# A fused attention and expert kernel: half tiles for the experts' x, and another order around the first two experts

## The chip, the cores and the metric

The kernel runs on one core of one Trainium2 chip. The metric is the device time of one execution in microseconds (us). Five engines work side by side, each through its own queue in order: TensorE (PE, whose weight loads are listed as PEld), VectorE (DVE), ScalarE (ACT), GpSimd (POOL) and SyncE (SP, which only issues DMAs here). They wait for one another through semaphores.

## The reference

Three stages follow one another, and only the last one is touched by the change.

```python
# stage 1: a linear attention with a decaying state, 4 x 8 heads, 768 steps, head size 48
# stage 2, on 3072 tokens of width 384
x = ((x @ w1) * (x @ w2)) @ w3 @ w_out
# stage 3: 8 experts, the best two for each token
noisy = x @ w_gate + log1p(exp(x @ w_noise)) * noise
top2 = argpartition(-noisy, 2)[:, :2]
top2_w = softmax(noisy[top2])
for e in range(8):
    h = maximum(x[mask_e] @ moe2_w1[e], 0)
    out[mask_e] += top2_w * (h @ moe2_w2[e])
```

## The kernel before, in words

The 3072 tokens are 24 chunks of 128, worked on in 12 groups of two. Attention of later chunks is interleaved with the projection of earlier groups: `mo_ab` makes the product of the two projections in four pieces (fp = 0 to 3), `mo_x` multiplies a piece by the folded w3·w_out (with the gate's 16 columns appended) into two banks of the accumulator memory, one for each chunk, and `mo_out` empties the banks: a copy of the gate's logits into `LZ` by DVE, a copy of x into `xo` by ACT, and a DMA of `xo` to a table of rows in memory. `gate_top` and `gate_put` turn the logits of four chunks into places (`slots`) in the experts' lists and write them there from POOL.

Every product is made of three matmuls (`mm3`, lines 171 to 173): each f32 operand is a rounded high part (h, a cast by ACT) and a rest (l, a subtraction by DVE), and h·h, h·l and l·h are added up.

An expert has up to 800 tokens in two halves: half 0 is four tiles of 128, half 1 is two tiles of 128 and a last one of 32. `load_idx` reads an expert's list (`ti`), `gather` fetches its rows (`xg`), `turn` writes them to `expert_rows` and reads them back through a transposing DMA into the tile `XTx` (for expert 0's first half the tile `XTa`), and `tr` splits that into `XTh` (three casts by ACT, line 749) and `XTl` (three subtractions by DVE, line 750). `mm1(hf, ff)` makes column block ff of the hidden layer from them, with a Relu by ACT and a rest by DVE behind it, and `mm2(e, j)` the output of tile j, which ACT scales (`ye`, line 799) and POOL adds to the output by an indirect DMA. `split_e(e, m, i)` splits quarter i of an expert's first (m = 0, `WAh`, `WAl`) or second (m = 1, `WBh`, `WBl`) weight matrix. The accumulator banks are `pb_66` to `pb_73`.

In the kernel before, `XTh`, `XTl` and, from expert 1 on, `XTx` are one tile each of 800 columns, and a half is a slice of it. For expert 0's second half the rows come too late for the way through memory; `tr_pe` joins them on DVE (`join`) and transposes them with nine matmuls on PE, put in the middle of the last of half 0's four `mm2`.

What sets the order: DVE's instructions stay in the order in which the program names them (`manual_schedule`). On the other engines a scheduler may move an instruction ahead of others that wait longer; one in `keep_in_program_order` stays behind the one that the program names just ahead of it on its engine, though later ones may still overtake it. So are kept all DMAs of SP, the casts of `tr`, and the casts of `split_e` for experts from 1 on. An instruction waits for every earlier one of the program whose tiles it needs, as the scheduler sees the overlap of the slices.

Around the change the program reads: last group, in whose steps i = 7 and i = 11 stand `turn(0, 0)` and `tr(0, 0)`; the last `mo_x` and `mo_out`; eight `mm1` of expert 0's half 0 with the last four chunks' gate in between (lines 898 to 916); four `mm2` with `tr_pe`; eight `mm1` of half 1; `turn(1, 0)` and `turn(1, 1)`; `mm2` of tiles 4, 6 and 5 with expert 1's first weights split behind them, and `tr(1, 0)` after tile 5 (j == NT - 2); then the loop over experts 1 to 7. In expert 1's first half, `turn(2, 0)` stands at ff = 3 and `tr(1, 1)` right behind it.

Of the kernel before, what the change touches and what calls it, by code (L numbers as in the profile page):

```python
# [18 lines left out]
P = 128  # L19
# [52 lines left out]
def tile_kernel(ctx: ExitStack, tc: tile.TileContext, dt, nat, w3t, wout, w1, w2, e1, e2, cf, ci, out):  # L72
# [462 lines left out]
    def mo_out(g):  # L535
        for tt in range(2):
            t = 2 * g + tt
            dve.tensor_copy(out=LZ[:, t, :], in_=bX[tt][:, DM:XW])
            xo = work.tile([P, 2 * DM], U16, name="xo")
            act.copy(out=halves(xo), in_=bX[tt][:, :DM].bitcast(U16).rearrange("p (d t) -> p t d", t=2))  # L540
            act.dma_start(out=x2d[DUMP + t * P:DUMP + P + t * P], in_=xo)
# [133 lines left out]
    def open_a():  # L675
        EP["a"] = ctx.enter_context(tc.tile_pool(name="epa", bufs=1))
        XT["h"] = EP["a"].tile([P, 3, CAP], F32R, name="XTh")
        XT["l"] = EP["a"].tile([P, 3, CAP], F32R, name="XTl")
        XT["x"] = EP["a"].tile([P, 3, NAB[0]], F32, name="XTa")
        open_h(EP["a"], 0)  # L680
# [9 lines left out]
    def open_b():  # L690
        EP["b"] = ctx.enter_context(tc.tile_pool(name="epb", bufs=1, side="right"))
        open_h(EP["b"], 1)
        XT["x"] = EP["b"].tile([P, 3, CAP], F32, name="XTx")
# [9 lines left out]
    def split_e(e, m, i):  # L703
        s = slice(768 * i, 768 * i + 768)
        o = 768 * (i % 2)
        src = RW[e, m, i // 2][:, o:o + 768]
        h, l = (WAh, WBh)[m][:, s], (WAl, WBl)[m][:, s]
        cast = act.copy(out=h, in_=src)  # L708
        if e:
            tc.keep_in_program_order(cast)  # L710
        dve.tensor_tensor(out=l, in0=src, in1=f(h), op=OP.subtract)
# [23 lines left out]
    def turn(e, hf):  # L735

        for j in range(TA) if hf == 0 else range(TA, NT):
            tc.keep_in_program_order(sp.dma_start(
                out=rows[e % 2, 2 * TPT * j:2 * TPT * j + 2 * rows_of(j)].rearrange("(p t) d -> p (t d)", t=2),
                in_=XG[e, j][:rows_of(j)]))  # L740
        a = 2 * hf * NAB[0]
        s = slice(a, a + 2 * NAB[hf])
        tc.keep_in_program_order(sp.dma_start_transpose(out=XT["x"].bitcast(U16)[:, :, s], in_=rows[e % 2, s]))

    def tr(e, hf):
        s = slice(hf * NAB[0], hf * NAB[0] + NAB[hf])
        for db in range(3):
            x, h = XT["x"][:, db, s], XT["h"][:, db, s]
            tc.keep_in_program_order(act.copy(out=h, in_=x))  # L749
            dve.tensor_tensor(out=XT["l"][:, db, s], in0=x, in1=f(h), op=OP.subtract)  # L750
# [7 lines left out]
    def tr_pe():  # L758
        for j in range(TA, NT):
            join(j)  # L760
        s = slice(NAB[0], NAB[0] + NAB[1])
        for db in range(3):
# [4 lines left out]
            split(XT["h"][:, db, s], XT["l"][:, db, s], bank[:, :NAB[1]])  # L767
# [4 lines left out]
    def mm1(hf, ff, banks=None):  # L772
        n = NAB[hf]
        s0 = hf * NAB[0]
        banks = banks or MB[:2 + hf]
        bank = banks[ff % len(banks)][:, :n]
        for kb in range(3):
            w = slice(kb * FF + ff * P, kb * FF + ff * P + P)
            mm3(bank, WAh[:, w], WAl[:, w], XT["h"][:, kb, s0:s0 + n], XT["l"][:, kb, s0:s0 + n], kb == 0, kb == 2)
# [60 lines left out]
    def first_half(e, r):  # L840
# [5 lines left out]
        for ff in range(8):  # L846
            mm1(0, ff)
            if ff in (3, 6) and e + 1 < E:
                turn(e + 1, ff // 6)
            if e == 1 and ff == 3:  # L850
                tr(1, 1)
# [20 lines left out]
    for g in range(NGRP):  # L872
# [7 lines left out]
        for i in range(12):  # L880
            if g == NGRP - 1 and i == 7:
                turn(0, 0)
            if g == NGRP - 1 and i == 11:
                tr(0, 0)
# [3 lines left out]
            elif g:  # L888
                mo_x(g - 1, 3)
                mo_out(g - 1)  # L890
# [12 lines left out]
    low_p()  # L903
    mo_x(NGRP - 1, 3)
    mo_out(NGRP - 1)
# [3 lines left out]
    for ff in range(8):  # L909
        for _ in range((5, 1, 0, 2, 1)[ff] if ff < 5 else 1):  # L910
            next(gen, None)
        mm1(0, ff, (bA, bB, PB[4], PB[5]))
# [21 lines left out]
    for i, j in enumerate((TA, NT - 1, *range(TA + 1, NT - 1))):  # L934
        mm2(0, j)
        split_e(1, 0, i)
        if j == NT - 2:
# [130 lines left out]
```

## Time and profile before

| what | us |
|---|---|
| median of 3 runs (lowest, highest) | 940.91 (940.27, 942.82) |
| the profiled execution, time | 944.25 |
| its span, which the views count in | 942.5 |
| PE busy in it | 902.0 (96%) |
| DVE busy | 493.0 (52%) |
| ACT busy | 429.6 (46%) |
| POOL busy | 243.6 (26%) |

The mean granted clock of PE over the span is 0.98 of its full speed. Matmuls are pipelined: a row's duration runs from its start to its modelled end, and the next one starts before that, so the pace of PE is read from the distance of starts. A row's bracket says how long the engine sat idle before it and which instruction ended that.

### The profile page before, as it was taken

The page shows a single profiled execution, that of the slowest core. Times are in us where ns is not written, and L with a number is a line of the kernel's source. Part 1 is how long each engine was busy: PE and PEld are TensorE (multiplying, and loading weights), DVE is VectorE, ACT ScalarE, POOL GpSimd, SP SyncE. Part 2 cuts the span into 40 slices and gives each one's busy share as a digit, 9 for nine tenths or more (in the row PEclk, how much of TensorE's full clock was granted, in tenths as well). Part 3 has the DMA queues.
Part 4 walks back from the last instruction along what each step waited for, and adds up shares of the span by engine and source line. Part 5 has one row for each costly group of instructions (what it writes and reads, how often), then busy time and mean ns, then how long its engine had stood idle before and what let it go on. Part 6 is the DMA issues. An engine that isn't in the chain of part 4 may idle for free.

```text
span 942.5 us, 17579 instructions
## 1 busy us (share of the span) xinstructions
PE 902.0 (96%) x7076; PEld 834.2 (89%) x7076; DVE 493.0 (52%) x1177; ACT 429.6 (46%) x875; POOL 243.6 (26%) x218
## 2 busy tenths in 40 slices
PE   8998999999999999999989978999999999999994
PEld 6787799999999999999978857989898999989894
DVE  5887874756756666655344344353343434353430
ACT  6777556456456545644451333343334343343320
POOL 2100001041141231231405540704224160613112
PEclk9998999999999999999999898999999999999998
DMA  9946377254253442420332982846748283854212
GB/s 355 363 143 209 134 86 218 88 133 163 97 166 122 136 127 80 125 80 19 105 97 88 184 257 60 241 103 167 178 117 210 76 213 73 224 120 95 26 21 36
DMA packets 96827, 130.41 MB, mean 138 GB/s; under 512 B 56064, under 2 KB 76768, under 8 KB 96736
## 3 DMA queue, kind: packets, MB, share of 16 engines
q1 hardware_dynamic: 81120, 104.76, 37.5%
q0 software_dynamic: 12160, 19.72, 11.1%
q10 hardware_dynamic: 3456, 4.72, 1.4%
q8 instruction: 57, 0.93, 0.4%
q14 instruction: 34, 0.28, 0.1%
HBM read 88.12 MB, written 31.66 MB: 127 GB/s over the span
## 4 chain that ended last, share of the span: by engine, by line
PE 78%; DVE 6%; issue 6%; DMA 5%; ACT 2%; POOL 2%; POOLq 0%; SPq 0%; DVEq 0%; ACTq 0%
PE pb L171 23%; PE pb L172 23%; PE pb L173 23%; PE pb L309 3%; PE pb L249 2%; DMA ti<-slots 1%; PE pb L804 1%; PE pb L270 1%; POOL slots L646 1%; DVE cvz L155 1%; PE pb L259 1%; DMA xg<-x_rows,ti 1%; ACT top L146 1%; DMA raw<-w 1%; POOL xg L732 1%
## 5 line engine op out<-in xcount | busy, mean ns | idle before, releaser
L809 POOL DMA_INDIRECT out<-ye,ti x56 | 89.1, 1592 | 255.4 <-ACT ye L799 231.6
L171 PE MATMUL pb<-XTh,WAh 128*128 128x512 f32 (+1 forms) x384 | 134.6, 351 | 10.5 <-ACT XTh L749 9.9
L172 PE MATMUL pb<-XTl,WAh 128*128 128x512 f32 (+1 forms) x384 | 133.5, 348 | 0.6 <-DVE XTl L750 0.6
L173 PE MATMUL pb<-XTh,WAl 128*128 128x512 f32 (+1 forms) x384 | 132.0, 346 | 0.0
L171 PE MATMUL pb<-WBh,HH 128*128 128x384 f32 x384 | 131.3, 342 | 0.4 <-ACT WBh L708 0.4
L173 PE MATMUL pb<-WBh,HH 128*128 128x384 f32 x384 | 130.4, 340 | 0.0
L172 PE MATMUL pb<-WBl,HH 128*128 128x384 f32 x384 | 130.3, 339 | 0.0
L781 ACT ACTIVATE HH<-pb 128x512 fp32r<-128x512 f32 (+1 forms) x128 | 62.8, 492 | 120.4 <-PE pb L173 118.8
L782 DVE SCALAR_TENSOR_TENSOR HH<-pb,HH 128x256 fp32r<-128x256 f32 (+1 forms) x128 | 71.1, 557 | 88.7 <-ACT HH L781 88.7
L799 ACT ACTIVATE ye<-pb,ti 128x384 f32<-128x384 f32 x48 | 27.9, 582 | 151.8 <-PE pb L173 112.7
L646 POOL DMA_INDIRECT slots<-g_sc,g_si x48 | 51.5, 1074 | 167.3 <-DVE g_si L645 85.2
L171 PEld LDWEIGHTS pb<-XTh,WAh 128*128 128x128 f32 x384 | 73.2, 191 | 21.0 <-ACT XTh L749 10.8
L171 PE MATMUL pb<-xh,WAh 128*128 128x256 f32 x288 | 82.3, 286 | 3.4 <-DVE W1l L125 3.1
L172 PE MATMUL pb<-xl,WAh 128*128 128x256 f32 x288 | 82.2, 285 | 0.9 <-DVE xl L316 0.9
L171 PE MATMUL pb<-xh,WBh 128*128 128x256 f32 x288 | 81.7, 284 | 0.9 <-DVE pp L515 0.5
L173 PE MATMUL pb<-xh,WAl 128*128 128x256 f32 x288 | 82.2, 285 | 0.0
L173 PE MATMUL pb<-xh,WBl 128*128 128x256 f32 x288 | 81.7, 284 | 0.3 <-DVE WBl L162 0.2
L172 PEld LDWEIGHTS pb<-XTl,WAh 128*128 128x128 f32 x384 | 73.2, 191 | 9.7 <-DVE XTl L750 1.5
L172 PE MATMUL pb<-xl,WBh 128*128 128x256 f32 x288 | 81.7, 284 | 0.0
L173 PEld LDWEIGHTS pb<-XTh,WAl 128*128 128x128 f32 x384 | 72.6, 190 | 8.2
L171 PEld LDWEIGHTS pb<-WBh,HH 128*128 128x128 f32 x384 | 72.6, 189 | 5.9 <-ACT WAh L708 4.4
L242 ACT ACTIVATE am<-cft,cc 128x128 f32<-128x128 f32 x192 | 61.2, 393 | 29.9 <-DVE cc L236 29.9
(173 smaller groups left out, 2034.6 us busy)
## 6 DMA issues: line engine op xcount, KB each, us to landing
dtc<-dt SPq DMA_DIRECT2D x24, 772.0 KB, 4.7
raw<-e SPq DMA_DIRECT2D x18, 768.0 KB, 6.2
raww<-e SPq DMA_DIRECT2D x14, 768.0 KB
nrk<-nat SPq DMA_DIRECT2D x24, 384.0 KB, 5.0
expert_rows<-xg SPq DMA_DIRECT2D x46, 192.0 KB, 5.7
rawf<-w3t SPq DMA_DIRECT2D x16, 512.0 KB, 5.9
nv<-nat SPq DMA_DIRECT2D x24, 256.0 KB, 2.8
raw<-w SPq DMA_DIRECT2D x8, 768.0 KB, 7.4
```

Of the source, the lines that this page charges most:

```text
L146: act.activation(out=t.bitcast(F16).rearrange("p (n t) -> p n t", t=2)[:, :, 1], in_=top, func=AF.Copy)
L171: pe.matmul(o, wh, xh, start=start, stop=False)
L172: pe.matmul(o, wh, xl, start=False, stop=False)
L173: pe.matmul(o, wl, xh, start=False, stop=stop)
L242: act.activation(out=AM[j][:, h], in_=ident, func=AF.Copy, scale=KS["c", j][:, h:h + 1])
L249: pe.matmul(bST[hb][:, P * a:P * a + P], KT[j][q, a].rearrange("p s i -> p (s i)"), RT[j][q, a].rearrange("p s i -> p (s i)"), start=True, ...
L309: pe.matmul(o, lt, rh, start=st, stop=en, tile_position=tp)
L646: ins = pool.indirect_dma_start(out=table, out_offset=bass.IndirectOffsetOnAxis(ap=si[:, i, k:k + 1], axis=0), in_=SC[:, i, k, :], in_offs ...
L781: act.activation(out=Hh[hf][:, ff], in_=bank[:, :n], func=AF.Relu)
L782: dve.scalar_tensor_tensor(Hl[hf][:, ff], bank[:, :n], 0.0, f(Hh[hf][:, ff]), op0=OP.max, op1=OP.subtract)
L799: act.activation(out=y[:n], in_=bank[:n], func=AF.Copy, scale=wt)
L809: ins = pool.indirect_dma_start(out=out, out_offset=bass.IndirectOffsetOnAxis(ap=ti(e, j)[:, 0:1], axis=0), in_=y[:n], in_offset=None, com ...
```

## The change

`mo_out` loses its copy of the logits to a function of its own, `mo_lz`, which stands ahead of it everywhere. `XTh`, `XTl` and `XTx` become two tiles each, one for a half, `XTx0` taking the place of `XTa` for all experts. `tr(0, 0)` moves from step 11 of the last group to behind its last `low_p`. The second chunk of the last `mo_out` moves into the loop of `mm1`, behind the first gate steps at ff = 0, with its copy kept in program order. The casts of expert 0's second weights are kept in program order too. `tr(1, 0)` stands after tile 6 instead of tile 5, and `tr(1, 1)` at ff = 2, ahead of `turn(2, 0)`. The lines that only follow the renaming are cut.

```diff
-    def mo_out(g):
+    def mo_lz(g):
         for tt in range(2):
+            dve.tensor_copy(out=LZ[:, 2 * g + tt, :], in_=bX[tt][:, DM:XW])
+
+    def mo_out(g, tts=(0, 1), pin=lambda x: x):
+        for tt in tts:
             t = 2 * g + tt
-            dve.tensor_copy(out=LZ[:, t, :], in_=bX[tt][:, DM:XW])
             xo = work.tile([P, 2 * DM], U16, name="xo")
-            act.copy(out=halves(xo), in_=...)
+            pin(act.copy(out=halves(xo), in_=...))
             act.dma_start(out=x2d[DUMP + t * P:DUMP + P + t * P], in_=xo)
...
-        XT["h"] = EP["a"].tile([P, 3, CAP], F32R, name="XTh")
-        XT["l"] = EP["a"].tile([P, 3, CAP], F32R, name="XTl")
-        XT["x"] = EP["a"].tile([P, 3, NAB[0]], F32, name="XTa")
+        for hf in range(2):
+            for k in "hl":
+                XT[k, hf] = EP["a"].tile([P, 3, NAB[hf]], F32R, name=f"XT{k}{hf}")
+        XT["x", 0] = EP["a"].tile([P, 3, NAB[0]], F32, name="XTx0")
...
-        XT["x"] = EP["b"].tile([P, 3, CAP], F32, name="XTx")
+        XT["x", 1] = EP["b"].tile([P, 3, NAB[1]], F32, name="XTx1")
...
         cast = act.copy(out=h, in_=src)
-        if e:
+        if e or m:
             tc.keep_in_program_order(cast)
...
         for ff in range(8):
             mm1(0, ff)
+            if e == 1 and ff == 2:
+                tr(1, 1)
             if ff in (3, 6) and e + 1 < E:
                 turn(e + 1, ff // 6)
-            if e == 1 and ff == 3:
-                tr(1, 1)
...
             if g == NGRP - 1 and i == 7:
                 turn(0, 0)
-            if g == NGRP - 1 and i == 11:
-                tr(0, 0)
...
             elif g:
                 mo_x(g - 1, 3)
+                mo_lz(g - 1)
                 mo_out(g - 1)
...
     low_p()
+    tr(0, 0)
     mo_x(NGRP - 1, 3)
-    mo_out(NGRP - 1)
+    mo_lz(NGRP - 1)
+    mo_out(NGRP - 1, (0,))
...
     for ff in range(8):
         for _ in range((5, 1, 0, 2, 1)[ff] if ff < 5 else 1):
             next(gen, None)
+        if ff == 0:
+            mo_out(NGRP - 1, (1,), tc.keep_in_program_order)
         mm1(0, ff, (bA, bB, PB[4], PB[5]))
...
         mm2(0, j)
         split_e(1, 0, i)
-        if j == NT - 2:
+        if j == NT - 1:
             tr(1, 0)
```

PE, at the seam between the last group's projection (`W1h`, `ph`, `pl`: its last piece) and expert 0's first `mm1`, before:

```order
L171 MATMUL pb_68<-W1h,ph 128x400
L172 MATMUL pb_68<-W1l,ph 128x400
L171 MATMUL pb_69<-W1h,ph 128x400
L172 MATMUL pb_69<-W1l,ph 128x400
L171 MATMUL pb_66<-XTh,WAh 128x512
L172 MATMUL pb_66<-XTl,WAh 128x512
L173 MATMUL pb_66<-XTh,WAl 128x512
L171 MATMUL pb_66<-XTh,WAh 128x512
L172 MATMUL pb_66<-XTl,WAh 128x512
L173 MATMUL pb_66<-XTh,WAl 128x512
L171 MATMUL pb_66<-XTh,WAh 128x512
L172 MATMUL pb_66<-XTl,WAh 128x512
```

The same place now:

```order
L172 MATMUL pb_68<-W1l,ph 128x400
L173 MATMUL pb_68<-W1h,pl 128x400
L171 MATMUL pb_69<-W1h,ph 128x400
L172 MATMUL pb_69<-W1l,ph 128x400
L173 MATMUL pb_69<-W1h,pl 128x400
L171 MATMUL pb_69<-W1h,ph 128x400
L172 MATMUL pb_69<-W1l,ph 128x400
L173 MATMUL pb_69<-W1h,pl 128x400
L171 MATMUL pb_66<-XTh_5857,WAh 128x512
L172 MATMUL pb_66<-XTl_5858,WAh 128x512
L173 MATMUL pb_66<-XTh_5857,WAl 128x512
```

The last piece's twelve matmuls stand together now and the first `mm1` behind them; before, eight of the twelve stood behind eight matmuls of the first `mm1`. On DVE, the subtraction that makes `pl` now stands ahead of the three that make `XTl`, instead of behind them. The gate's three small matmuls stood behind four `mm1` and two matmuls of the first `mm2`; now they stand behind three `mm1`.

ACT, at the end of expert 0, where expert 1's first weights (`WAh`) and the first half of its x (`XTh`) are cast, before:

```order
L708 CAST WAh<-raww 128x768
L799 ACTIVATE ye<-pb_68,ti_6345 128x384 [waits DMASW7_49,PE_49,Activation_49]
L708 CAST WAh<-raww 128x768 [waits DMAHW6_49]
L749 CAST XTh<-XTx 128x512 [waits DMAHW6_49]
L749 CAST XTh<-XTx 128x512 [waits DMAHW2_49]
L749 CAST XTh<-XTx 128x512
```

The same place now:

```order
L712 CAST WAh<-raww 128x768
L752 CAST XTh_5857<-XTx_5861 128x512 [waits DMAHW6_49]
L752 CAST XTh_5857<-XTx_5861 128x512 x2
L800 ACTIVATE ye<-pb_68,ti_6347 128x384 [waits DMASW7_49,PE_49,Activation_49]
L712 CAST WAh<-raww 128x768 x2
```

The three casts of x stood behind the scaling (`ye`) of expert 0's last tile and the third quarter of the weights; now they stand ahead of that `ye`.

ACT, in expert 1's first half, from the cast of the first quarter of its second weights on (HH: the Relu of a block), before:

```order
L708 CAST WBh<-raw_6693 128x768 [waits DMAHW3_49]
L781 ACTIVATE HH_5860<-pb_66 128x512 [waits PE_49]
L781 ACTIVATE HH_5860<-pb_67 128x512 [waits PE_49]
L781 ACTIVATE HH_5860<-pb_66 128x512 [waits PE_49]
L781 ACTIVATE HH_5860<-pb_67 128x512 [waits PE_49]
L708 CAST WBh<-raw_6693 128x768
L749 CAST XTh<-XTx 128x288 [waits DMAHW6_49,Activation_49]
```

The same place now:

```order
L782 ACTIVATE HH_5862<-pb_66 128x512 [waits PE_49]
L782 ACTIVATE HH_5862<-pb_67 128x512 [waits DVE_49,PE_49]
L712 CAST WBh<-raw_6695 128x768 [waits DMAHW3_49]
L782 ACTIVATE HH_5862<-pb_66 128x512 [waits PE_49]
L752 CAST XTh_5859<-XTx_6346 128x288 [waits DMAHW2_49,Activation_49]
L752 CAST XTh_5859<-XTx_6346 128x288 [waits Activation_49] x2
L782 ACTIVATE HH_5862<-pb_67 128x512 [waits PE_49]
```

The casts of x's second half stood behind the Relus of blocks 2 to 5 and the second quarter of the weights, which the scheduler had let overtake them, and waited for another DMA than now (DMAHW6 and DMAHW2 are counters of SP's DMAs); now they stand behind the Relu of block 2.

## Rows read from the trace of the kernel before

**Rows 1.** The page, its first line.
```profile
span 942.5 us, 17579 instructions
```

**Rows 2.** The timeline of PE, 477 to 485 us: start, duration, engine, line, operation, count, [idle before].
```profile
477.79 0.34 PE L172 MATMUL pb<-W1l,ph 128*128 128x400 f32 x1
479.43 0.50 PE L171 MATMUL pb<-XTh,WAh 128*128 128x512 f32 x1 [1.30 <-ACT XTh L749]
480.16 0.50 PE L172 MATMUL pb<-XTl,WAh 128*128 128x512 f32 x1 [0.23 <-DVE XTl L750]
481.54 0.63 PE L171 MATMUL pb<-XTh,WAh 128*128 128x512 f32 x1
484.89 0.40 PE L173 MATMUL pb<-XTh,WAl 128*128 128x512 f32 x1
```

**Rows 3.** The timeline of PE, 491 to 502 us.
```profile
491.33 0.51 PE L171 MATMUL pb<-WBh,HH 128*128 128x384 f32 x2
493.05 0.50 PE L171 MATMUL pb<-XTh,WAh 128*128 128x512 f32 x1 [0.61 <-DVE HH L782]
501.64 0.34 PE L172 MATMUL pb<-WBl,HH 128*128 128x384 f32 x1
```

**Rows 4.** The timeline of DVE, 479 to 518 us.
```profile
479.41 1.90 DVE L750 TENSOR_TENSOR XTl<-XTa,XTh 128x512 fp32r<-128x512 f32 x3 [3.41 <-ACT XTh L749]
491.33 0.19 DVE L584 TENSOR_TENSOR g_mb<-g_M 128x32 bf16<-128x32 f32 x1
516.84 1.80 DVE L754 COPY xg<-xg 128x768 uint16<-128x768 uint16 x3 [11.87 <-issue]
```

**Rows 5.** The timeline of ACT, 486 to 568 us.
```profile
486.50 0.24 ACT L556 ACTIVATE g_t<-g_t 128x32 f32<-128x32 f32 x1
544.78 0.58 ACT L799 ACTIVATE ye<-pb,ti 128x384 f32<-128x384 f32 x1 [3.06 <-issue]
545.98 1.66 ACT L749 CAST XTh<-XTx 128x512 fp32r<-128x512 f32 x3
567.96 1.10 ACT L749 CAST XTh<-XTx 128x288 fp32r<-128x288 f32 x3 [6.64 <-DMA XTx<-expert_rows]
```

**Rows 6.** The timeline of PE, 515 to 526 us.
```profile
515.87 0.33 PE L173 MATMUL pb<-WBh,HH 128*128 128x384 f32 x1
517.65 0.33 PE L766 MATMUL pb<-cft,xg 128*128 128x128 f32 x1 [1.45 <-DVE xg L754]
518.70 1.98 PE L766 MATMUL pb<-cft,xg 32*128 32x32 f32 x7 [0.21 <-DVE xg L754]
525.87 0.29 PE L171 MATMUL pb<-XTh,WAh 128*128 128x288 f32 x1
```

**Rows 7.** Two stretches: length, busy us of PE, PEld, DVE, ACT, POOL, granted clock, DMA.
```profile
481.00:483.00 2.00, 2.00 (x7) 1.67 (x6) 0.91 (x2) 1.56 (x2) 0.00 (x0) 0.56 0.00 0
519.00:521.00 2.00, 2.00 (x7) 1.21 (x8) 0.92 (x2) 1.08 (x3) 1.59 (x2) 0.50 0.88 114
```

**Rows 8.** The timeline of PE, 546 to 552 us.
```profile
546.65 0.73 PE L171 MATMUL pb<-XTh,WAh 128*128 128x512 f32 x2 [1.96 <-ACT XTh L749]
551.51 0.39 PE L171 MATMUL pb<-XTh,WAh 128*128 128x512 f32 x1
```

**Rows 9.** The timeline of SP's queue, 531 to 566 us.
```profile
531.42 4.54 SPq L743 DMA_TRANSPOSE XTx<-expert_rows  x1
539.07 1.46 SPq L743 DMA_TRANSPOSE XTx<-expert_rows  x1
562.73 3.11 SPq L743 DMA_TRANSPOSE XTx<-expert_rows  x1
```

**Rows 10.** The timeline of PE, 561 to 574 us.
```profile
561.37 0.45 PE L171 MATMUL pb<-WBh,HH 128*128 128x384 f32 x1 [0.35 <-ACT WBh L708]
568.44 0.61 PE L171 MATMUL pb<-XTh,WAh 128*128 128x288 f32 x1 [6.62 <-ACT XTh L749]
573.51 0.39 PE L171 MATMUL pb<-XTh,WAh 128*128 128x512 f32 x1
```

More of the change, by code (lines that the diff above doesn't have):

```diff
@@ L533, in mo_x @@
                 mm3(bX[tt][:, :XW], PH[g, fp][:, s], PL[g, fp][:, s], wh, wl, ff == 0, ff == 7)
-    def mo_out(g):
+    def mo_lz(g):
         for tt in range(2):
+            dve.tensor_copy(out=LZ[:, 2 * g + tt, :], in_=bX[tt][:, DM:XW])
+    def mo_out(g, tts=(0, 1), pin=lambda x: x):
+        for tt in tts:
             t = 2 * g + tt
-            dve.tensor_copy(out=LZ[:, t, :], in_=bX[tt][:, DM:XW])
             xo = work.tile([P, 2 * DM], U16, name="xo")
-            act.copy(out=halves(xo), in_=bX[tt][:, :DM].bitcast(U16).rearrange("p (d t) -> p t d", t=2))
+            pin(act.copy(out=halves(xo), in_=bX[tt][:, :DM].bitcast(U16).rearrange("p (d t) -> p t d", t=2)))
             act.dma_start(out=x2d[DUMP + t * P:DUMP + P + t * P], in_=xo)
@@ L742, in turn @@
         s = slice(a, a + 2 * NAB[hf])
-        tc.keep_in_program_order(sp.dma_start_transpose(out=XT["x"].bitcast(U16)[:, :, s], in_=rows[e % 2, s]))
+        tc.keep_in_program_order(sp.dma_start_transpose(out=XT["x", hf].bitcast(U16), in_=rows[e % 2, s]))
     def tr(e, hf):
-        s = slice(hf * NAB[0], hf * NAB[0] + NAB[hf])
         for db in range(3):
-            x, h = XT["x"][:, db, s], XT["h"][:, db, s]
+            x, h = XT["x", hf][:, db], XT["h", hf][:, db]
             tc.keep_in_program_order(act.copy(out=h, in_=x))
-            dve.tensor_tensor(out=XT["l"][:, db, s], in0=x, in1=f(h), op=OP.subtract)
+            dve.tensor_tensor(out=XT["l", hf][:, db], in0=x, in1=f(h), op=OP.subtract)
     def join(j):
@@ L760, in tr_pe @@
             join(j)
-        s = slice(NAB[0], NAB[0] + NAB[1])
         for db in range(3):
@@ L766, in tr_pe @@
                 pe.transpose(bank[:, o:o + n], XG[0, j][:n, P * db:P * db + P], ident[:n, :n])
-            split(XT["h"][:, db, s], XT["l"][:, db, s], bank[:, :NAB[1]])
+            split(XT["h", 1][:, db], XT["l", 1][:, db], bank[:, :NAB[1]])
     MB, MC, AD = (bA, bB, bK), [1], [-1]
@@ L773, in mm1 @@
         n = NAB[hf]
-        s0 = hf * NAB[0]
         banks = banks or MB[:2 + hf]
@@ L778, in mm1 @@
             w = slice(kb * FF + ff * P, kb * FF + ff * P + P)
-            mm3(bank, WAh[:, w], WAl[:, w], XT["h"][:, kb, s0:s0 + n], XT["l"][:, kb, s0:s0 + n], kb == 0, kb == 2)
+            mm3(bank, WAh[:, w], WAl[:, w], XT["h", hf][:, kb], XT["l", hf][:, kb], kb == 0, kb == 2)
         n = (TA, TB)[hf] * TPT
```

## The prediction

> **What bounds the kernel now.** The first line of the page [rows 1] and the table of busy times say that PE works 96% of the span of 942.5 us. So PE's own idle stretches are what a change of order can win. I then read PE's timeline for brackets, engine by engine backwards from each, and the table of stretches for the granted clock. Between 477 and 574 us four places stand out; the reader is to see in each when the last matmul ahead of it started, when work went on, and at which pace. A matmul of 512 columns goes at 0.23 us: 28 of them start from 484.89 to 491.33 [rows 2, 3]. One of 384 columns goes at 0.176: 82 start from 501.64 to 515.87 [rows 3, 6]. One of 288 I take in proportion to the 512, at 0.13.
>
> The four places: PE waits 1.30 and 0.23 for `XTh` and `XTl` of expert 0 [rows 2], and works at half rate after that, with matmuls 0.43 apart around 481.54 and a granted clock of 0.56 in 481 to 483 [rows 2, 7]. It waits 1.45 and 0.21 for the joined rows [rows 6], with a granted clock of 0.50 in 519 to 521 [rows 7], that is 1.2 of 2.4 GHz. It waits 1.96 for expert 1's first half of x [rows 8]. And it waits 6.62 for its second half [rows 10]. That last one is the key to the change: the casts waited for a transposing DMA into `XTx` until 567.96 [rows 5]; the DMA that brings this half was issued at 539.07, and the only one issued between is that of expert 2's first half at 562.73 [rows 9], which landed 5.2 us later, just when the casts began. So these casts waited for the other half of the same tile, with nothing of it to read. I look for no fifth place: the experts from 2 on keep their order.
>
> **Term A, the seam and the gate.** Before, PE's next start after 477.79 was due at 477.97 (0.18 for 400 columns, by proportion); `mm1` was over and `mm2` under way at 501.64, with two matmuls (0.35) of that done early [rows 2, 3], so the work took until 501.29. Now all twelve matmuls of the last piece come first. Their `pl` has its place in DVE's idle 3.41 us ahead of 479.41 [rows 4], so eight more go through by 479.44, where `XTh` is ready anyhow (479.43); `XTl` holds the second `mm1` matmul until 480.16 and the third until 480.50 as before [rows 2]. Twenty-five more at 0.23 end three blocks at 486.25. Then the gate's matmuls, in PE's order now behind three blocks, must wait. Their chain starts with the logits behind `XTl` on DVE at 479.41 + 1.90 = 481.31 [rows 4]. Two copies and one small operation of 0.1 to 0.2, and on ACT one copy of `xo` in front of it (768 elements, about 0.8 by the cast of 512 in 1.66 / 3 [rows 5]), put the exponential at 482.1, against 486.50 [rows 5]: 4.4 earlier. All that follows on DVE and ACT is the same chain: `g_mb` is made at 486.9 instead of 491.33 [rows 4], and the gate's matmuls are over at 488.04 (493.05 less its idle 0.61, less 4.4) [rows 3]. Forty-five more matmuls of 512 columns take 10.35; for the last small gate matmul, which waits for DVE again, I allow 0.6, as much as the bracket of 0.61 [rows 3]. So 499.0 against 501.29: 2.3 won. The pinned casts of the second weights now follow the Relus of blocks 4 to 7, and their cover is `mm1` itself: the last is wanted 18 matmuls of 384 columns into `mm2`, 3.2 us after 499.0, and ACT and DVE need about 0.8 and 0.95 behind the last Relu (768 columns, by the 512 of [rows 5] and [rows 4]); if that cover fails, each us late costs one. The second `xo` goes to memory at about the same time as before, and the gathers that read it wait for the slots much longer. Bounds: if the clock falls at the new wait as it fell at 481, the same 3.4 us at half rate (481.5 to 484.9 [rows 2]) cost 1.7, so 0.6; without any wait at the gate 4.5.
>
> **Term B, the join.** The slots, POOL's eight writes, the list, the gathers and the join at 516.84 [rows 4] stand behind one another, and all wait for the gate: 4.4 earlier, 512.4. PE comes to the transposes 2.3 earlier, at 513.75 instead of 516.05 (515.87 [rows 6] and one pace). The third transpose, the last one held by a join, started at 518.70 [rows 6] and now can at 514.3. Lead 4.3 to 4.4, of which 2.0 are new. From there to 525.87 [rows 6] 7 transposes, 12 matmuls of 384 and 6 of 288 took 7.17; at full rate 1.98 (left as it is) + 2.11 + 0.78 = 4.87. So 2.3 more if the clock stays up, which I take, as the long idle time ahead of its fall is gone. Bounds for the two together: 0 (the DMAs no earlier, the clock as before) and 4.7.
>
> The Trainium skill has a rule against this ("TensorE: Matmul & The Clock Gate", Part 4, PE-mode transpose): a transpose on PE does not count as PE being busy for its clock. The trace can't decide, since idle time and nine transposes stood together when the clock fell. By that rule the 2.3 would not come, and the time would be that of the first rival below.
>
> **Term C, expert 1's first half of x.** Before, from 544.53 (the idle 1.96 ahead of 546.65, and one pace of overlap) 18 matmuls of 512 columns took until 551.51 [rows 8]: 6.98. Now ACT casts x ahead of the last `ye`, in the 3.06 us that it sat idle before 544.78 [rows 5], so `XTh` is there before PE wants it; DVE follows while PE works on tile 5. The third quarter of the weights still comes behind that `ye`, at about 545.3 to 546.1 (544.78 + 0.58, and 0.8), and PE needs it for the seventh or eighth matmul: just in time. Eighteen at 0.23 are 4.14, and 0.2 for one bank late: 2.6 won. The condition is that the transposing DMA has landed: it was issued at 531.42 for 4.54 [rows 9], and landed about 2.1 after that as at 562.73 + 3.11 + 2.1 = 567.9, so 538.1; with the gate's 4.4 it is 533.7, and ACT comes to the casts at 541.7 less A and B, 6.6: 535.1. Bounds 1.0 and 2.8.
>
> **Term D, expert 1's second half of x.** With tiles of their own, and with the casts named ahead of `turn(2, 0)`, nothing holds them: their DMA was issued 29 us before they ran. The casts (1.10 [rows 5]) and DVE's subtractions stand now behind block 2, where a block's 9 x 0.23 = 2.07 cover them on either engine. PE goes on at 561.6 instead of 568.44: 6.8. From there to 573.51 [rows 10] 9 matmuls of 288 and 6 of 512 took 5.07 against 2.55 at full rate: 2.5. Together 9.3; bounds 6.6 (the clock falls for another reason) and 9.7.
>
> What is late next? Expert 2's rows, transposed at 562.73 and landed at 567.9, are wanted in the middle of expert 1's second `mm2`, some 30 us later; a PE that is 9 us sooner doesn't reach them. Expert 1's second weights are loaded when a matmul of tile 6 frees their buffer, and that moves with PE; C alone brings their first use nearer, by 2.6. Nothing of this is given back later, as every later expert is bound by PE.
>
> **The sum.** 2.3 + 2.0 + 2.3 + 2.6 + 9.3 = 18.5; I take off 0.8 for small waits at new seams: 17.7. The profiled execution, 944.25 with 1.75 outside its span, would come to 926.5. It lies 3.3 above the median of the runs shown, so the forecast is 940.91 - 17.7 = 923.2, rounded to 923.
>
> **The rivals.**
> - The clock falls all the same, at the transposes (2.3 less), at the gate's new wait (1.7 less), or both. For it: it fell three times after waits of 1.3 and more [rows 2, 6, 10]. Against it: after 1.96 [rows 8] it didn't, matmuls going on 0.23 apart there. 924.9 to 927.2.
> - The change doesn't do what it says in D: the casts still wait for a DMA of expert 2 or for the list behind it, so that 9.3 shrinks to 0 to 2. For it: the wait was a matter of the scheduler's view of slices. Against it: in ACT's order they now wait for another counter of SP's DMAs. 931 to 933.
> - Slower: the first half's DMA lands late. Now its casts stand in ACT's queue ahead of `ye`, so the last tile's output, the weights' casts and all Relus queue behind them, and PE with them. Each us of landing after 535.1 costs one; it turns the whole gain and the bound of 2.8 into a loss from a landing 20.5 us late on, at 555.6. For it: the DMA engines are crowded by weight loads there. Against it: before, it had landed by 545.98, when the casts ran [rows 5]. 944 and more.
>
> **How the numbers follow.** Forecast (921 to 924.9) 0.52, first rival 0.33, second 0.09, slower 0.02, some cover lost that I don't see with no net change 0.04. The bounds added up give gains from 8.2 to 21.7, times from 919.2 to 932.7; the range of 8 in 10 is 919 to 930, cutting off most of the second rival. What can be told from no change is about 0.3%, 2.8 us: faster 0.93, same 0.05, slower 0.02.
>
> **What would show it.** In the profile after: D, no bracket above 1 us on a matmul with `XTh` of 288 columns in expert 1, and the casts behind block 2 without a DMA as releaser; C, the first `mm1` of expert 1 following the last `mm2` within 0.5 us; A, the exponential of the last gate 2.7 us after the first `mm1` matmul (before, 7.1), and a bracket of about 1 us on the gate's matmul instead of on `XTh`; B, the first transpose within 0.3 us of the matmul ahead, and a granted clock of 1.0 behind the transposes. The forecast is wrong if the waits go and the time moves by less than 10, or if a later expert's matmuls show brackets that they hadn't.

## The result, and the profile after

The changed kernel takes 925.57 us (median of 4 runs, 924.98 to 928.57) against 941.79 for the kernel before in the same set (940.27 to 942.82): a ratio of 0.9835, 95% interval 0.9808 to 0.9863, that is 16.2 us less. The forecast was 17.7 less and 923.0, in a range of 919 to 930. A later set gave 0.9840 (0.9819 to 0.9862).

The profiled execution took 928.57, its span is 926.8 against 942.5 [rows 1], 15.7 less. The page's first line:

```profile
span 926.8 us, 17584 instructions
```

The seam, in PE's timeline of the changed kernel (start, duration, engine, line, operation, count, [idle before]):

```profile
474.70 0.35 PE L171 MATMUL pb<-W1h,ph 128*128 128x400 f32 x1
...
476.71 0.34 PE L173 MATMUL pb<-W1h,pl 128*128 128x400 f32 x1
477.08 0.49 PE L171 MATMUL pb<-XTh,WAh 128*128 128x512 f32 x1
...
484.85 0.18 PE L603 MATMUL pb<-g_mb,trib 128*128 128x32 bf16 x1 [0.73 <-DVE g_mb L587]
485.52 0.18 PE L604 MATMUL pb<-g_cm,oneb 128*128 128x32 bf16 x1 [0.49 <-DVE g_cm L590]
```

The 1.30 of [rows 2] are gone: the last piece's matmul at 476.71 is followed by `mm1` at 477.08. The wait has moved to the gate's matmuls, 0.73 and 0.49, where about one us was expected. ACT and DVE show the gate's chain, and ACT what follows in expert 1:

```profile
476.41 1.66 ACT L752 CAST XTh<-XTx 128x512 fp32r<-128x512 f32 x3 [2.29 <-DMA XTx<-expert_rows]
479.77 0.23 ACT L559 ACTIVATE g_t<-g_t 128x32 f32<-128x32 f32 x1
...
533.94 1.66 ACT L752 CAST XTh<-XTx 128x512 fp32r<-128x512 f32 x3 [1.98 <-DMA XTx<-expert_rows]
...
544.91 0.83 ACT L712 CAST WBh<-raw 128x768 fp32r<-128x768 f32 x1 [4.53 <-DMA raw<-e]
545.64 0.59 ACT L782 ACTIVATE HH<-pb 128x512 fp32r<-128x512 f32 x1
546.13 1.09 ACT L752 CAST XTh<-XTx 128x288 fp32r<-128x288 f32 x3
```

```profile
484.60 0.19 DVE L587 TENSOR_TENSOR g_mb<-g_M 128x32 bf16<-128x32 f32 x1
510.06 1.75 DVE L757 COPY xg<-xg 128x768 uint16<-128x768 uint16 x3 [11.06 <-DMA xg<-x_rows,ti]
```

The exponential stands 2.69 behind the first `mm1` matmul (before, 486.50 - 479.43 = 7.07 [rows 2, 5]); the join is at 510.06 and not at 516.84 [rows 4]. From `mm2` of expert 0 (496.45) on, PE:

```profile
496.45 0.34 PE L171 MATMUL pb<-WBh,HH 128*128 128x384 f32 x1
...
511.06 0.34 PE L173 MATMUL pb<-WBh,HH 128*128 128x384 f32 x1
511.24 1.95 PE L768 MATMUL pb<-cft,xg 128*128 128x128 f32 x9
515.32 0.29 PE L171 MATMUL pb<-XTh,WAh 128*128 128x288 f32 x1
...
530.50 0.45 PE L171 MATMUL pb<-WBh,HH 128*128 128x384 f32 x1
...
534.60 0.34 PE L173 MATMUL pb<-WBh,HH 128*128 128x384 f32 x1
534.78 0.40 PE L171 MATMUL pb<-XTh,WAh 128*128 128x512 f32 x1
535.34 0.50 PE L172 MATMUL pb<-XTl,WAh 128*128 128x512 f32 x1 [0.17 <-DVE XTl L753]
...
539.76 0.50 PE L171 MATMUL pb<-XTh,WAh 128*128 128x512 f32 x1
...
547.39 0.80 PE L171 MATMUL pb<-XTh,WAh 128*128 128x512 f32 x1 [3.16 <-DVE HH L783]
...
557.17 0.29 PE L171 MATMUL pb<-XTh,WAh 128*128 128x288 f32 x1
...
571.21 0.53 PE L805 MATMUL pb<-raw,HM 128*32 128x384 f32 x4
```

The nine transposes follow without a bracket (1.45 and 0.21 in [rows 6]); expert 1's first `mm1` follows the last `mm2` in one pace (1.96 in [rows 8]); its second `mm1` at 557.17 follows in one pace too (6.62 in [rows 10]). One bracket is new: 3.16 in expert 1's first `mm1`. Stretches of the same trace, to be read for the granted clock (the third number from the end, in front of the DMA share and GB/s):

```profile
481.00:483.00 2.00, 2.00 (x10) 1.62 (x9) 1.04 (x5) 1.97 (x3) 0.00 (x0) 1.00 0.15 53
513.00:515.00 2.00, 2.00 (x13) 1.96 (x13) 0.94 (x3) 0.48 (x2) 1.39 (x3) 1.00 0.58 185
547.00:549.00 2.00, 1.61 (x4) 1.33 (x5) 2.00 (x5) 0.72 (x2) 1.12 (x1) 0.50 0.82 341
```

At 481 and behind the transposes the clock stays at 1.00 (0.56 and 0.50 in [rows 7]); at 547, behind the new wait, it is 0.50 (and 0.68 in 549 to 551), so the wait costs 3.16 and some 1.5 to 2 of half rate. What PE waited for there is a chain: its bank and `HH` come from a Relu, that Relu stands on ACT behind the cast of expert 1's second weights, and the cast waited 4.53 for their load. SP's queue says why the load was late:

```profile
523.88 6.37 SPq L747 DMA_TRANSPOSE XTx<-expert_rows  x1
530.35 1.49 SPq L742 DMA_DIRECT2D expert_rows<-xg  x3
535.36 1.62 SPq L747 DMA_TRANSPOSE XTx<-expert_rows  x1
537.07 1.00 SPq L705 DMA_DIRECT2D raw<-e  x2
```

The load (L705) went out at 537.07. The matmuls of tile 6 had freed its buffer by 530.50, when `mm2` went on behind them (540.26 before); but on SP it stands behind both transposes. The first of these started 7.5 earlier than before (523.88 against 531.42 in [rows 9]), but is on the queue for 6.37 and not 4.54. The second waits for the rows written behind the first to land, 3.5 us after the writes at 530.35 were over, and started only 3.7 earlier (535.36 against 539.07). The load and its first use in the kernel before, SP's queue and then ACT:

```profile
540.62 1.01 SPq L701 DMA_DIRECT2D raw<-e  x2
```

```profile
552.20 0.83 ACT L708 CAST WBh<-raw 128x768 fp32r<-128x768 f32 x1
```

Milestones of PE in the two traces, and what each stretch saved. The rows of before for it that stand nowhere else are these, and with them 540.26, the matmul behind tile 6 of expert 0:

```profile
477.23 0.35 PE L171 MATMUL pb<-W1h,ph 128*128 128x400 f32 x1
524.62 0.44 PE L171 MATMUL pb<-XTh,WAh 128*128 128x288 f32 x1
540.26 0.45 PE L171 MATMUL pb<-WBh,HH 128*128 128x384 f32 x1
588.00 1.50 PE L804 MATMUL pb<-raw,HM 128*32 128x384 f32 x16
```

| | before | after | difference | saved since the row above |
|---|---|---|---|---|
| first of the last piece's twelve matmuls | 477.23 | 474.70 | 2.53 | 2.53, ahead of the change |
| second `mm1` of expert 0 | 524.62 | 515.32 | 9.30 | 6.77: A and B |
| third block of expert 1's first `mm1` | 551.51 | 539.76 | 11.75 | 2.45: C 1.99, 0.46 in expert 0 |
| tile 6 of expert 1 | 588.00 | 571.21 | 16.79 | 5.04: D less the new wait |
| end of the span | 942.5 | 926.8 | 15.7 | -1.1 |

The first 2.53 are not of the change: in the trace of before, PE's first matmuls behind its warm-up started 0.2 to 0.5 later and some casts of the first weights later still, by 70 us into the span it was 2.35, and it stayed so. The granted clock in 10 to 20 us was 0.83 there and 1.00 in the changed kernel's trace. Either comes with either kernel: of all fourteen traces, the five with 0.66 to 0.89 in that stretch, two of them of kernels with the changed seam, reach the last piece at 476.7 or later, and the nine with 1.00, before_again among them, at 475.5 or earlier. The 1.1 at the end is about 0.2 in each of the experts 2 to 7, spread over their first `mm1`; I have no cause for it.

### The profile page after: what moved, and what is told of

Its sections match the earlier page's. It is cut to its first block, busy times and chain, and to the rows that moved or that the text cites. A ratio compares the mean times of both kernels' runs of the same rounds, so it can differ in the third digit from the quotient of the medians.

```text
span 926.8 us, 17584 instructions
## 1 busy us (share of the span) xinstructions
PE 894.5 (97%) x7076; PEld 827.4 (89%) x7076; DVE 493.0 (53%) x1177; ACT 429.1 (46%) x875; POOL 244.3 (26%) x218
## 4 chain that ended last, share of the span: by engine, by line
PE 79%; DVE 6%; issue 5%; DMA 4%; ACT 3%; POOL 2%; SPq 1%; POOLq 0%; DVEq 0%; ACTq 0%
PE pb L171 24%; PE pb L172 23%; PE pb L173 23%; PE pb L309 4%; PE pb L249 2%; POOL slots L649 1%; PE pb L270 1%; PE pb L805 1%; DMA raw<-e 1%; DVE cvz L155 1%; PE pb L259 1%; ACT top L146 1%; SPq L747 1%; DMA slots<-g_sc,g_si 1%; DMA raw<-w 1%
## 5 line engine op out<-in xcount | busy, mean ns | idle before, releaser
L782 ACT ACTIVATE HH<-pb 128x256 fp32r<-128x256 f32 (+1 forms) x128 | 62.8, 492 | 113.3 <-PE pb L173 112.0
```

What stands on the lines that cost most here:

```text
L782: act.activation(out=Hh[hf][:, ff], in_=bank[:, :n], func=AF.Relu)
```

## The experiments

Twelve runs followed, two of them of the unedited kernels, in four sets, each with runs of the kernel before beside them. Ratios are to those; the kernel before took 943.5 to 945.8 in them. Where nothing else is said, a diff is against the changed kernel. The last column is PE's idle time in one stage of one trace; where it is large, the text calls it the stall.

| kernel | median us | ratio (95%) | PE idle in expert 0's second `mm1` |
|---|---|---|---|
| changed, first set | 925.57 | 0.9835 (0.9808-0.9863) | 0 |
| weights_first | 933.05 | 0.9873 (0.9840-0.9907) | 2.1 |
| split_late | 930.80 | 0.9847 (0.9815-0.9879) | 3.7 |
| tiles_no_move | 928.81 | 0.9840 (0.9808-0.9873) | 2.1 |
| move_no_tiles | 938.26 | 0.9935 (0.9908-0.9962) | 3.2 |
| changed_again | 930.23 | 0.9840 (0.9819-0.9862) | 3.2 |
| own_buffer | 932.07 | 0.9863 (0.9842-0.9885) | 0 |
| seam_undone | 934.71 | 0.9887 (0.9866-0.9909) | 2.1 |
| c_undone | 933.89 | 0.9889 (0.9868-0.9909) | 2.2 |
| before_again | 942.80 (one) | - | 2.4 |
| no_scatter | 926.79 | 0.9810 (0.9782-0.9839) | 0 |
| late_adds | 930.00 | 0.9845 (0.9821-0.9869) | 0.9 |
| late_adds_split | 927.39 | 0.9814 (0.9791-0.9837) | 0 |

**weights_first**

```
     turn(1, 0)
-    turn(1, 1)
...
         if j == NT - 1:
             tr(1, 0)
+            load_e(1, 1, 0)
+            load_e(1, 1, 1)
+            turn(1, 1)
     split_e(1, 0, 3)
-    load_e(1, 1, 0)
-    load_e(1, 1, 1)
```

> The changed kernel, with expert 1's second weights issued on SP's queue right behind the transpose of expert 1's first half, ahead of the rows and the transpose of its second half. Theory (queue order): the load goes out at about 530.6, when PE's matmuls of tile 6 have freed the buffer and SP is through its first transpose, instead of at 537.07; it lands 7.8 later, at 538.4, and ACT's cast of it, wanted at 540.4, no longer waits 4.53. The 3.16 us that PE sat idle and the half clock behind them (together about 5.0) go: 920.6 us. The second half of x then lands at about 540 to 541, just ahead of its casts at 542. Rival (crowding): the load takes 7.8 us because transposes, gathers and other loads share the DMA engines, and an earlier issue lands hardly earlier, or x's second half lands late in its place: 924 to 926.

Neither theory: no faster than the changed kernel; whether it is slower is open, as the intervals overlap. ACT no longer waits for the weights, but it waits 2.56 for x's second half, which landed some 10 us later than expected:

```profile
545.55 0.83 ACT L712 CAST WBh<-raw 128x768 fp32r<-128x768 f32 x1
...
550.58 0.77 ACT L752 CAST XTh<-XTx 128x288 fp32r<-128x288 f32 x2 [2.56 <-DMA XTx<-expert_rows]
```

And PE came to expert 1 at 540.5 and not at 534.78: 2.4 of it stood there already at expert 0's second `mm1` (517.76 against 515.32), and the other 3.3 is a stall in that `mm1`, with 2.1 idle in one bracket, that neither of the first two traces has. The clock stayed at 1.00 behind it. So in this trace SP's order only decides which of the two transfers is late; what the new wait for the weights costs can't be judged beside this stall.

**split_late**

```
-            if ff in (1, 5):
-                split_e(e, 1, ff // 4)
+            if ff in ((4, 5) if e == 1 else (1, 5)):
+                split_e(e, 1, int(ff == 5))
```

> The changed kernel, with SP's queue as it is, but ACT's cast of the first quarter of expert 1's second weights put behind block 4 of the first mm1, not behind block 1, so that Relus and x's casts no longer stand behind it. Theory: the wait is one of ACT's queue for a load that lands at 544.9; at block 4 PE is at about 546, the load has landed, and the 5.0 us go as well: 920.6 us. Rival: what PE lacked was not the Relu behind that cast but the x casts or the banks, and the time stays at 925 to 926.

No wait in expert 1, and no gain in time: the stall stands in front here too (3.7). Inconclusive as a test of the wait.

**tiles_no_move**, and against the kernel before **move_no_tiles**

```
-            if e == 1 and ff == 2:
-                tr(1, 1)
             if ff in (3, 6) and e + 1 < E:
                 turn(e + 1, ff // 6)
+            if e == 1 and ff == 3:
+                tr(1, 1)
```

> The changed kernel, with the casts of expert 1's second half of x back behind block 3 and behind the issue of expert 2's first transpose; the halves keep tiles of their own. Theory: the tiles alone take the wait for the other half's DMA away, so within 1 us of the changed kernel, 925 to 927, no wait for a DMA on these casts. Rival: the place alone does it; then the casts wait for expert 2's transpose again, some 6 to 9 us on PE, 931 to 935.

> The kernel before, with one edit: the casts of expert 1's second half of x are named behind block 2, ahead of expert 2's first transpose; tiles are shared as before. Theory: the place alone is also enough, since the transpose into the other half is then named later; the 6.62 us and the half clock behind them go, 9.3: 932.5. Expert 1's second weights come before they are wanted here, as C has not brought their use nearer, so no new wait. Rival: only tiles of their own help, 941 to 942.

Either edit alone takes the wait of 6.62 away. ACT's casts in the two, first tiles_no_move:

```profile
549.19 1.09 ACT L752 CAST XTh<-XTx 128x288 fp32r<-128x288 f32 x3
```

and move_no_tiles:

```profile
559.85 1.09 ACT L749 CAST XTh<-XTx 128x288 fp32r<-128x288 f32 x3
```

No DMA releases these casts in either. With the tiles the ratio is that of the changed kernel, as the theory said; the 928.81 lies outside its 925 to 927, in a set whose kernel before took 943.45. The move alone gave 5 to 6 us and not 9.3; before_again bears on the reason.

**changed_again**: the changed kernel, nothing edited.

> The changed kernel itself, on the same chip as the runs beside it, since the kernel before was about 2 us slower in the last set than in the first. Ratio to the kernel before 0.983 to 0.985. What the last four traces leave open: three of them, which have the changed seam and casts of x, stall in expert 0's second mm1 (PE idle 2.1 to 3.7 and then the half clock) where the changed kernel's trace does not, with the Relus 1 to 3 us behind the recorded end of their block. Theory: this stall is not of these edits, and comes here too; PE is then some 4 to 5 us later at expert 1, and its second weights come in time. Rival: it is of these edits, and this trace has the wait for the weights and no stall.

The theory held for the stall and for the weights; PE was 7.0 later at expert 1, not 4 to 5. Of the three earlier traces that it names, the half clock follows the stall only in tiles_no_move (0.50 in 527 to 529); in weights_first and split_late it stays at 1.00. ACT in expert 0's second `mm1`, then PE, and a stretch behind the stall:

```profile
519.67 0.38 ACT L782 ACTIVATE HH<-pb 128x256 fp32r<-128x256 f32 x1 [2.28 <-PE pb L173]
...
525.50 0.38 ACT L782 ACTIVATE HH<-pb 128x256 fp32r<-128x256 f32 x1 [3.91 <-remote]
```

```profile
526.49 0.40 PE L171 MATMUL pb<-XTh,WAh 128*128 128x288 f32 x1 [2.84 <-DVE HM L785]
...
541.74 0.40 PE L171 MATMUL pb<-XTh,WAh 128*128 128x512 f32 x1
...
572.96 1.50 PE L805 MATMUL pb<-raw,HM 128*32 128x384 f32 x16
```

```profile
527.00:531.00 4.00, 4.00 (x21) 4.00 (x20) 1.52 (x7) 1.41 (x4) 0.00 (x0) 0.57 1.31 121
```

The Relu at 525.50, the third block's, ran 5.2 us after the recorded end of its block (520.33) and 3.9 after the Relu ahead was over (521.59); in the first two traces a Relu of this stage follows its block's end by 0.03 to 0.04. The bracket's releaser, "remote", is no engine or DMA that the profile names. PE then lacked the bank, and went on at a clock of 0.57. No wait for the second weights follows: PE came to expert 1 at 541.74 instead of 534.78, and from there to tile 6 it took 31.2 us, where the first trace took 36.4 (534.78 to 571.21). So the new wait costs 5.2 where PE is early, and nothing where the stall has made PE late.

**own_buffer**

```
+        elif m == 1 and e == 1:
+            rw = EP["b"].tile([P, 1536], F32, name="rawe", bufs=2)
...
+    load_e(1, 1, 0)
+    load_e(1, 1, 1)
     turn(1, 0)
     turn(1, 1)
...
-    load_e(1, 1, 0)
-    load_e(1, 1, 1)
```

> The changed kernel, with a buffer of its own for expert 1's second weights, so that both halves are issued on SP ahead of the rows of expert 1, at about 508 us, not behind its second transpose at 537. Theory (queue order): they land before 525 and ACT's cast at 540 waits for nothing. If expert 0's second mm1 does not stall, 5.0 us less than the changed kernel; if it does, PE is late there already and about 0 to 1 less. Rival (crowding): 1.5 MB more beside the gathers of 505 to 520 make the rows of expert 0 or 1 later, and PE waits there: 1 to 4 us more than the changed kernel.

The rival: 1.8 us more, and all five runs lie above all five of changed_again in the same set. ACT's cast waits for nothing, but PE waits for the joined rows; that the load beside the gathers makes these late is the rival's explanation, and this one trace fits it:

```profile
513.43 0.33 PE L770 MATMUL pb<-cft,xg 128*128 128x128 f32 x1 [1.80 <-DVE xg L759]
515.06 0.33 PE L770 MATMUL pb<-cft,xg 128*128 128x128 f32 x1 [1.31 <-DVE xg L759]
```

The clock is at 0.50 to 0.51 from 516 to 522, and PE reaches the second `mm1` at 521.6. There is no stall behind that, and it isn't known why: PE came there later still in move_no_tiles (522.8) and seam_undone (524.6), and stalled.

**seam_undone**

```
+            if g == NGRP - 1 and i == 11:
+                tr(0, 0)
...
-    tr(0, 0)
     mo_x(NGRP - 1, 3)
-    mo_lz(NGRP - 1)
-    mo_out(NGRP - 1, (0,))
+    mo_out(NGRP - 1)
...
-        if ff == 0:
-            mo_out(NGRP - 1, (1,), tc.keep_in_program_order)
...
-        if e or m:
+        if e:
```

> The changed kernel with the seam as before: expert 0's casts named before the last three pieces, the last logits copied behind no cast of x, the second copy of x and the casts of the second weights not pinned. Tiles and the order in expert 1 stay changed. Theory: A and B go (2.3 + 4.3), but PE is then later at expert 1 and its second weights come in time, which gives back up to 5: between 1.6 and 6.6 us more than the changed kernel; PE shows the 1.3 and 1.5 us of idle time and the half clock at 481 and 519 again. Rival: the seam gives nothing by itself, since the wait for the slots sets the time: 0 to 1 more.

4.5 us more than changed_again, inside the theory's 1.6 to 6.6. Its PE shows the old wait, and the clock of the stretch behind it:

```profile
480.24 0.50 PE L171 MATMUL pb<-XTh,WAh 128*128 128x512 f32 x1 [1.50 <-ACT XTh L749]
```

```profile
481.00:483.00 2.00, 2.00 (x5) 1.61 (x6) 1.72 (x3) 0.91 (x2) 0.00 (x0) 0.51 0.22 89
```

**c_undone**

```
-        if j == NT - 1:
+        if j == NT - 2:
             tr(1, 0)
```

> The changed kernel with the casts of expert 1's first half of x behind tile 5 again, not behind tile 6. Theory: C (2.0 to 2.6) comes back as a wait of about 2 us on the first mm1 of expert 1, and as much of the wait for the second weights goes, as these stand on SP's queue at the same time: 0 to 1 us more than the changed kernel. Rival: C is independent of that wait, 2 to 2.6 more.

3.7 us more than changed_again in the medians, 2.2 in the two profiled executions: the rival, or more, since there was no wait for the weights left to give back. The trace also shows the half clock behind the transposes of expert 0, which changed_again's doesn't. PE has its wait again, and 0.34 at the matmul behind it:

```profile
543.30 0.73 PE L171 MATMUL pb<-XTh,WAh 128*128 128x512 f32 x2 [1.96 <-ACT XTh L752]
```

**before_again**: the kernel before, nothing edited, for a trace.

> The kernel before, for a trace from the chip of the last sets, where it took 943.5 to 944.6 and not 941.8. Theory: the stall in expert 0's second mm1 (Relus 1 to 4 us behind the recorded end of their block, PE idle 2 to 4 us, then half clock) is not of the change, and shows here too, while the wait of 6.62 us in expert 1 is a little shorter or the same. Rival: it is of the change's seam, which brings PE to that place 9 us earlier beside the gathers of expert 1, and this trace has none.

The theory held, save that the wait in expert 1 is less than half as long, not a little shorter. Its PE has the stall as well (1.00 and 1.43), and after it this wait is 2.87, not 6.62:

```profile
566.28 0.61 PE L171 MATMUL pb<-XTh,WAh 128*128 128x288 f32 x1 [2.87 <-ACT XTh L749]
```

So D's wait, which ends with a DMA, is worth less where the stall has made PE late. From expert 1's first `mm1` to its tile 6 this trace took 39.2 and move_no_tiles 32.9, so D was 6.3 between these two, about what move_no_tiles gave. For the changed kernel the stall takes the wait for the second weights away too. The ratios of the two sets, 0.9835 and 0.9840, agree, though the traces show different terms: A and B together 6.8 in the first pair and 4.3 between before_again and changed_again, and from there to tile 6 of expert 1 7.5 and 8.8.

**no_scatter** (split_late, and):

```
+        if e == 0 and j < TA:
+            return
         ins = pool.indirect_dma_start(out=out, ...
```

> The changed kernel with the cast of expert 1's second weights behind block 4 (as in split_late), and with the first four additions of expert 0's output left out: their rows are never added to the output, and POOL and the DMA engines have that much less to do from 508 to 527 us. Theory (the stall comes with the indirect transfers beside it): the Relus of expert 0's second mm1 follow their blocks within 0.5 us, PE does not stall there, and as the wait for the weights is gone too the time is about 5 us under split_late's ratio: 0.979 to 0.980. Rival (other traffic, or none of it): the stall stays, 0.984 to 0.985.

Half of the theory: no idle time in expert 0's second `mm1`, but the Relus do not follow within 0.5 us; three of them were 1.4, 1.7 and 0.8 late. Its ratio, 0.9810, is 0.001 above what was expected. The kernel leaves work out, and its interval (0.9782 to 0.9839) overlaps that of split_late.

**late_adds**

```
-        ins = pool.indirect_dma_start(out=out, ...
+        if e == 0 and j < TA:
+            HELD.append((j, y, n))
+        else:
+            put(e, j, y, n, ti(e, j))
...
         if j == NT - 1:
             tr(1, 0)
+            tj = EP["a"].tile([P, TA, 2], I32, name="tj")
+            dve.tensor_copy(out=tj, in_=TI[0, 0])
+            for jj, y, n in HELD:
+                put(0, jj, y, n, tj[:, jj])
```

> The changed kernel, with expert 0's first four additions to the output issued on POOL behind its other three, at about 536 to 545 us and not at 508 to 525; no work is left out. (Their index goes through one small copy on DVE, so that they can't come earlier, and there are eight buffers for the output's tiles, not six.) Theory (the additions beside the gathers make the stall in expert 0's second mm1): the stall goes, PE is 4 to 5 us earlier at expert 1, and then it depends on the second weights: in the run without these additions they were issued at 532.05, 5 us earlier than in the changed kernel, as the rows land sooner; so no wait for them, and a ratio of 0.979 to 0.981 to the kernel before. Rival: with PE earlier, the wait for the second weights takes the stall's place (3 us of idle time and the half clock), and the ratio stays at 0.983 to 0.985. Second rival: the additions disturb the casts and transposes of 536 to 545 as much, 0.984 or more.

**late_adds_split** is the same with the edit of split_late.

> As late_adds, with ACT's cast of expert 1's second weights behind block 4 too (split_late). Theory: no stall and no wait for the second weights in any case, 0.979 to 0.981; equal to late_adds within 0.001 if the weights come in time there, and 0.004 to 0.005 less if they don't. Rival: the second one of late_adds, 0.984 or more.

In both traces the stall shrinks (0.9, and none), though Relus were still up to 2.3 and 1.7 late, and SP's queue is sooner in its unchanged order. In late_adds_split:

```profile
523.70 3.29 SPq L747 DMA_TRANSPOSE XTx<-expert_rows  x1
...
530.09 1.45 SPq L747 DMA_TRANSPOSE XTx<-expert_rows  x1
531.63 1.00 SPq L705 DMA_DIRECT2D raw<-e  x2
```

The first transpose is on the queue for 3.29 and not 6.37, and the load goes out 5.4 us earlier than in the first trace of the changed kernel. Its clock stays up where changed_again had 0.57:

```profile
527.00:531.00 4.00, 4.00 (x26) 3.62 (x28) 0.52 (x2) 0.17 (x1) 0.00 (x0) 1.00 0.75 205
```

Expert 1's tile 6 comes at 567.97, against 572.96 in changed_again and 571.21 in the first trace. late_adds_split's runs (926.98 to 928.13) all lie below those of changed_again (929.14 to 930.76, another set on the same chip); their ratios, 0.9814 and 0.9840, have intervals that overlap. It is the fastest full kernel here, by about 2.5 us if that holds. late_adds alone has the time of the changed kernel, and so misses its theory's 0.979 to 0.981, though its one trace, of its fastest execution, has neither wait nor stall to speak of. The two kernels differ only in the place of ACT's cast of the second weights, and in their common set all five runs of late_adds_split lie below all five of late_adds, 2.6 us in the medians. That would fit a wait for the second weights in the executions that weren't traced; no trace shows it.

## Why the prediction was right, point by point

- **What bounds the kernel**: held. The four waits were the four to win, and the experts from 2 on kept their order, save for 0.2 us each.
- **A**: 2.3 predicted, 2.3 measured: from the last piece's first matmul to the first of `mm2`, 501.29 (of the working) - 477.23 = 24.06 against 496.45 - 474.70 = 21.75. Both sides of it came as named: the wait moved to the gate, 1.22 in two parts, and the clock didn't fall. seam_undone shows A and B together by undoing them, with 4.5 for the two in a set where the stall was there. What A wins by the clock doesn't come in every execution: in before_again PE idled 1.11 at the seam and the clock stayed at 1.00 in 476 to 482, and from the last piece to expert 0's second `mm1` it took 45.98, changed_again 41.70: 4.3 for A and B, not 6.8.
- **B**: 4.3 predicted, 4.46 measured (6.77 less 2.31). The first rival, that the clock falls at the transposes all the same, did not come in the changed kernel's trace: it was 1.00 behind them (0.50 before [rows 7]). The Trainium skill's rule ("TensorE: Matmul & The Clock Gate", Part 4, PE-mode transpose), that a transpose doesn't count as PE being busy for the clock, would have cost 2.3 here; it didn't, but the traces leave the rule open. Nine transposes of 1.95 us right behind a matmul left the clock at 1.00, and so did the idle 1.96 of [rows 8]. In c_undone two idle times of 0.31 and 0.30 at the same transposes were enough for a fall, and it shows 0.52 behind them, while changed_again (0.26, 0.23 and 0.15) and tiles_no_move (0.43) show 1.00 there:

```profile
517.00:519.00 2.00, 2.00 (x8) 2.00 (x8) 0.00 (x0) 0.00 (x0) 1.60 (x2) 0.52 0.64 163
```

- **C**: 2.6 predicted, 1.99 measured; c_undone gives 2.3 of idle time for it. The 18 matmuls took 4.98 (534.78 to 539.76) where 4.34 were forecast. Half of that is the condition: x was forecast landed by 533.7 and ACT free for the casts at 535.1. ACT was there earlier, and waited 1.98 for the DMA until 533.94, so that `XTl` came late: PE's second matmul began at 535.34, 0.56 behind the first where the pace is 0.23. The slower rival's mechanism thus did begin to bite, mostly behind PE's work on tile 5. The rest is spread over the two blocks.
- **D**: 9.3 predicted. The false wait went, by either of its two edits, and the casts have no DMA as releaser. Net 5.04 came. With the 5.2 of the new wait added back, D is 10.2. Where the stall stood in front of it, it was 6.3 (before_again and move_no_tiles).
- **The step that failed** is in "What is late next?", which put the cost of the next late transfer at nothing: "Expert 1's second weights are loaded when a matmul of tile 6 frees their buffer, and that moves with PE". The buffer did come free 9.8 us earlier (540.26 to 530.50), but the load stands on SP's queue behind two transposes that wait for gathered rows and landings, and it went out only 3.6 us earlier (540.62 to 537.07), while its first use came 11.8 us earlier (552.20 to 540.38, when ACT was free for it). In [rows 9] the transposes stand there; I read them for x alone, and not for what is queued behind them. weights_first bears it out in part: issued ahead of the second transpose, the load landed in time, and x was late in its place. What is missing by the step, 5.2, was made up in part by the 2.53 of the profiled pair that are no part of the change, by D's 0.9 more, and by the 0.8 taken off.
- **The allowance and the range**: the time lies 2.6 above the forecast, inside 919 to 930, and just outside the likeliest case's own range, whose upper end was 924.9. It lies in the first rival's 924.9 to 927.2, but not by that rival's mechanism: in the changed kernel's trace the clock stayed up at the transposes and at the gate. That the sum comes so near is in part luck: 2.53 of the 15.7 between the two profiled executions stood there before the change begins, and how much of that the medians hold isn't known; in most of the later traces the stall stands in the place of the new wait. "A gain of less than 10" didn't come. A later expert's bracket didn't come either.

What is not settled: why PE's completed blocks are seen late in expert 0's second `mm1`, and why only in some executions. That the four additions beside the gathers feed it is likely, not shown. In the three traces without them there, a Relu is at most 1.7 to 2.3 us late, against 3.8 to 5.6 in the eight traces with a stall of over 2 us; but the first two traces (0.04) and own_buffer (0.6) have the additions there and no stall.

## What to carry to other kernels

A wait taken away on the busiest engine brings the next use of every queue nearer: for each load behind it, ask what frees its buffer and also what stands ahead of it on the queue that issues it, and how much of that moves along. A transposing DMA into half of a tile can hold readers of the other half; a tile for each half, or readers named ahead of it, are both enough. When an edit shows no gain, look in the trace for a stall ahead of the place: a wait that ends with a transfer is worth only what PE isn't already late.

## What the runs showed of the hardware

- Relus that wait for PE's block ran late after the recorded end of that block, in all of the twelve later traces: at most 0.6 us in own_buffer, up to 5.6 in split_late, against 0.03 to 0.04 in the first two. In eight of the twelve PE was idle over 2 us for it. All these Relus stand between 519 and 535 us, beside gathers and the rows' writes, and but for three traces the additions to the output (DMA share 1.03 in 519 to 523 of changed_again). PE's matmuls were recorded at their usual pace up to the stall; their ends are modelled.
- The transposing DMA of expert 1's first half occupied SP's queue for 3.22 (late_adds) to 6.37 us (the changed kernel's first trace); what is queued behind it goes out later by that.
- The length of PE's idle time alone didn't tell whether the clock fell. It fell to about half after idle times of 3.16 (547), 2.84 (527, changed_again) and 1.50 (481, seam_undone), as in [rows 7], and once after 0.31 and 0.30 around transposes; it did not after the 0.73 and 0.49 at the gate, nor after 2.10 in weights_first. The idle 1.96 ahead of expert 1 left it at 1.00 in the trace of before [rows 8], and was followed by 0.50 in 548 to 550 in before_again.
